# Block-causal attention followed by RWKV channel mix: queries kept in four classes from the scores to the normalization

## The chip, the cores and the metric

The kernel runs on one core of a Trainium2 chip. The metric is the time of one execution on the device, in microseconds (us). Before the change it is 314.23 us, the median of three executions (314.18 to 315.11 us). The profile is one execution, with a span of 312.8 us from the first to the last instruction.

Engines go by the names of the profile: PE is TensorE's matrix multiply, PEld its weight load, DVE is VectorE, ACT is ScalarE, POOL is GpSimd, and SP is SyncE, which issues the transfers. L657 means line 657 of the kernel.

## The reference

Two layers, one after the other. Inputs are float32; q, k and v have the shape (8 batches, 8 heads, 576 tokens, 64).

```python
# attention, causal in blocks of 64 tokens
scores = q @ k.T / sqrt(64)                       # 576 x 576 for each batch and head
scores = where(block(i) >= block(j), scores, -1e9)
attn   = exp(scores - max);  attn /= attn.sum(-1) + 1e-9
x      = attn @ v                                 # heads side by side: (8, 576, 512)

# channel mix
x_prev = x shifted by one token
xk = mu_k * x + (1 - mu_k) * x_prev
xr = mu_r * x + (1 - mu_r) * x_prev
out = sigmoid(xr @ w_r) * (relu(xk @ w_k)**2 @ w_v)   # (8, 576, 512)
```

The kernel takes no maximum off the scores, and it normalizes after the product with v: it computes the sums of the exponentials ("den") and the unnormalized values ("num") on PE, and multiplies num by 1/den on the way from PSUM to SBUF.

## The kernel before

Work is done per batch `b` and pair of heads `pr`. Scores are held transposed: keys on partitions, queries along the columns. Of the 576 queries the first 512 (`CUT`) are handled in `J = 4` classes: query 4p + j has position p (0 to 127) and class j. The last 64 are a block of their own. `M = 128` positions, `WD = M + 64`.

Two layouts of the transposed queries exist. In batches 0 and 1 (`b < TURNED`) PE does the transposing and the queries lie in token order, p outer and j inner. In batches 2 to 7 a transfer does it, and they lie in class order, j outer and p inner. Scores are always written to PSUM in token order:

```python
LATER = [                     # three score steps of one pair: (column, key chunk, first and last position)
    [(0, 0, 0, M)],                                   # 512 columns
    [(0, 0, M, WD), (D, 1, 32, M), (448, 1, M, WD)],  # 64, 384, 64
    [(0, 2, H2, M), (256, 2, M, WD), (320, 3, 96, M), (448, 3, M, WD)],   # 256, 64, 128, 64
]                             # batch 0 has 256+128+256+256+256+128 columns of the first kind, 1280 too
...
for p, col, kc, a, z in mms:
    for h in range(2):                       # the two heads, on partitions 0-63 and 64-127
        ...
        if a < M:
            moving = ask[:, J * a:J * z]
            dst = PS[:, h, col:col + J * w]
            if b >= TURNED:
                moving = ask[:, 0:CUT].rearrange("d (j p) -> d p j", j=J)[:, a:z]
                dst = dst.rearrange("k (p j) -> k p j", j=J)
            nc.tensor.matmul(dst, keys, moving, start=True, stop=True)      # L657
        else:
            nc.tensor.matmul(PS[:, h, col:col + D], keys, ask[:, CUT:S],    # L660
                             start=True, stop=True)
```

So in batches 2 to 7 consecutive columns of the moving operand are 128 bf16 elements, 256 bytes, apart.

ACT takes the exponential of two heads by 512 columns at a time into the float16 tile `e` (L679), POOL clears the part that the causal mask cuts off (L688), and PE makes sums and values from `e`, four heads side by side in four groups of 32 output columns (all through L721):

```python
def probs(b, head, kc, a, z):        # columns of e for the positions a to z
    ...
    return E[:, J * (a - a0):J * (z - a0)]

def sums(PS, a, z):                  # class j of head g goes to the partitions of its group that FOURTH picks
    for j in range(J):
        for kc in kcs:
            lo = max(a, kc * 32)
            for g in range(G):
                tiled(PS[:, lo - a:z - a], FOURTH[:, (J - j) % J:(J - j) % J + R],
                      probs(b, 4 * Q + g, kc, lo, z)[:, j::J], g, ...)
    ...                              # and the last 64 queries, with ONES

def part(PS, xs, a, z):              # values: 512 columns for each x, even and odd channels
    ...
    ps = ps[:, J * (lo - a):J * (z - a)]
    tiled(ps, V[:, kc, 4 * Q + g, x:D:2], probs(b, 4 * Q + g, kc, lo, z), g, ...)
```

In the sums the moving operand is every fourth float16 of `e`, 8 bytes apart. In the values it is contiguous. DVE then turns the sums into reciprocals, spreads the four classes over the partitions, and normalizes:

```python
nc.vector.reciprocal(tiles["c", key][:, 0:z - a], PS[:, 0:z - a])            # L772
nc.vector.reciprocal(tiles["rd", key][:, CUT:S], PS[:, M:WD])                # L775
...
for j in range(J):                                                          # L781
    nc.vector.stream_shuffle(tiles["rd", key][:, J * a + j:J * z:J],
                             tiles["c", key][:, 0:z - a], [j] * 32)
...
nc.vector.tensor_tensor(x, num, r.unsqueeze(1).to_broadcast(...), ALU.mult)  # L825, 512 tokens
nc.vector.tensor_tensor(x, num[:, 0:n * D]..., r[:, CUT:S]..., ALU.mult)     # L817, last 64
```

The spread writes each class into every fourth float32 of `rd`, 16 bytes apart. `x` is the float32 tile `xt` in token order, from which the channel mix follows: differences (L897), mixes (L910), the three products on PE (L948, L983, L1014).

The order of all instructions is fixed when the kernel is built, by a small planner that goes by an estimated duration for each step.

Of the kernel before, what the change touches and what calls it, by code (L numbers as in the profile page):

```python
# [20 lines left out]
TURNED = 2  # L21
# [259 lines left out]
def kernel(  # L281
# [24 lines left out]
    M = CUT // J  # L306
    WD = M + D
    JT = S // D
    CH = 512
    CHUNKS = [(0, CH // 2), (CH // 2, CH // 2)] + [  # L310
        (i * CH, CH) for i in range(1, B * S // CH)]
# [303 lines left out]
    def add_score(b, pr, i):  # L615


        sbuf = plan.buf("s")
        tail = i is None
        Q = pr // 2  # L620
        takes, uses = [sbuf], [tiles["qktbuf", b]]
        if tail:
            takes.append(el_buf[b][Q])
            deps = sum([evac[x, b, pr + y] for x in ("qkt", "tail")
                        for y in range(2)], [])
            if b:
                deps.append(ready["l", b - 1, Q])
            mms = [(pr + x, x * D, J, M, WD) for x in range(2)]
        else:
            mms = [(pr,) + p for p in pieces(b)[i]]  # L630
            deps = evac["qkt", b, pr] + (
                evac["tail", b, pr] if any(p[3] == M for p in mms) else [])
            if i == 0:
                tiles["ebuf", b, pr] = plan.buf("e")
                takes.append(tiles["ebuf", b, pr])
            else:
                uses.append(tiles["ebuf", b, pr])

        def fn():
            qkt = tiles["qkt", b]  # L640
            PS = tiles["ps", b, pr, i] = new("s", [P, 2, 512], FP)
            if i == 0:
                tiles["e", b, pr] = new("e", [P, 2, 3, 512], F16)
            for p, col, kc, a, z in mms:
                for h in range(2):
                    rows = slice(h * D, h * D + D)
                    keys, ask = qkt[rows, p, 1], qkt[rows, p, 0]
                    w = z - a
                    keys = keys[:, kc * P:kc * P + P]
                    if a < M:  # L650
                        moving = ask[:, J * a:J * z]
                        dst = PS[:, h, col:col + J * w]
                        if b >= TURNED:
                            moving = ask[:, 0:CUT].rearrange(
                                "d (j p) -> d p j", j=J)[:, a:z]
                            dst = dst.rearrange("k (p j) -> k p j", j=J)
                        nc.tensor.matmul(dst, keys, moving, start=True,  # L657
                                         stop=True)
                    else:
                        nc.tensor.matmul(PS[:, h, col:col + D], keys,  # L660
                                         ask[:, CUT:S], start=True, stop=True)
        pe = on("PE", 0.06 if tail else 0.215 + 0.02 * i, fn, deps, takes, uses,
                name=f"s{b}t{Q}" if tail else f"s{b}{pr}{i}", mode="rows",
                steps=2 * len(mms))
        if tail:
            def exl():
                nc.scalar.activation(
                    E4s[b % 2][0:D, 4 * Q:4 * Q + 4].rearrange(
                        "p (h a) q -> p h a q" if b < TURNED else
                        "p (a h) q -> p h a q", h=2),  # L670
                    tiles["ps", b, pr, i][0:D, :, 0:2 * D].rearrange(
                        "p h (a q) -> p h a q", q=D), AF.Exp, scale=ISQ)
            ready["l", b, Q] = on("ACT", 0.27, exl, [pe],
                                  uses=[sbuf, el_buf[b][Q]])
            return
        ebuf = tiles["ebuf", b, pr]

        def ex():
            nc.scalar.activation(tiles["e", b, pr][:, :, i, :],  # L679
                                 tiles["ps", b, pr, i], AF.Exp, scale=ISQ)  # L680
        t = on("ACT", 0.905, ex, [pe] + ([ready["x", b, pr, 0]] if i else []),
               uses=[sbuf, ebuf])
        ready["x", b, pr, i] = t

        def zero():
            for col, kc, a, z in pieces(b)[i]:
                if a == kc * 32 and a < M:
                    nc.gpsimd.memset(  # L688
                        tiles["e", b, pr][D:P, :, i, col:col + D], 0.0)
        n = sum(a == kc * 32 and a < M for col, kc, a, z in pieces(b)[i])  # L690
        if n:
            ready["z", b, pr, i] = on("POOL", 0.15 * n, zero, [t], uses=[ebuf])

    def probs(b, head, kc, a, z):


        if kc == J:
            return E4s[b % 2][:, head]
        i, col, a0, z0 = [
            (i, col, a0, z0) for i, piece in enumerate(pieces(b))  # L700
            for col, k0, a0, z0 in piece if k0 == kc and a0 <= a and z <= z0][0]
        pr, h = place(b, head)
        E = tiles["e", b, pr][:, h, i, col:]
        if a == M:
            return E[:, 0:D]
        return E[:, J * (a - a0):J * (z - a0)]

    def add_values(b, Q):

# [14 lines left out]
        def sums(PS, a, z):  # L724
            kcs = [kc for kc in range(J) if kc * 32 < z]
# [3 lines that stand above are left out]
                    for g in range(G):  # L729
                        tiled(PS[:, lo - a:z - a],  # L730
                              FOURTH[:, (J - j) % J:(J - j) % J + R],
                              probs(b, 4 * Q + g, kc, lo, z)[:, j::J], g,
                              (j, kc) == (0, kcs[0]), (j, kc) == (J - 1, kcs[-1]))
            for kc in range(J + 1) if z == M else ():
                for g in range(G):
                    tiled(PS[:, M:WD], ONES, probs(b, 4 * Q + g, kc, M, WD), g,
                          kc == 0, kc == J)

        def part(PS, xs, a, z):
            V = VOs[b % 2]  # L740
            wide = J * (z - a) if a < M else D
            for n, x in enumerate(xs):
                cols = slice(n * wide, n * wide + wide)
                kcs = [kc for kc in range(J) if kc * 32 < z] + [J] * (a == M)
                for kc in kcs:
                    lo = max(a, kc * 32)
                    for g in range(G):
                        ps = PS[:, cols]
                        if a < M:
                            ps = ps[:, J * (lo - a):J * (z - a)]  # L750
                        tiled(ps, V[:, kc, 4 * Q + g, x:D:2],
                              probs(b, 4 * Q + g, kc, lo, z), g,
                              kc == kcs[0], kc == kcs[-1])

        def group(name, a, z, deps, steps, dur, r_dur, s_dur):
# [11 lines left out]

            def recip():
                tiles["c", key] = new("c", [P, M], FP)
                tiles["rd", key] = new("rd", [P, S], FP)  # L770
                PS = tiles["den", key]
                nc.vector.reciprocal(tiles["c", key][:, 0:z - a],  # L772
                                     PS[:, 0:z - a])
                if z == M:
                    nc.vector.reciprocal(tiles["rd", key][:, CUT:S],  # L775
                                         PS[:, M:WD])
            t = on("DVE", r_dur, recip, [t], takes=[cbuf, rd], uses=[dbuf])

            def spread():
                for j in range(J):  # L780
                    nc.vector.stream_shuffle(  # L781
                        tiles["rd", key][:, J * a + j:J * z:J],
                        tiles["c", key][:, 0:z - a], [j] * 32)
            return rd, on("DVE", s_dur, spread, [t], uses=[cbuf, rd]), key

# [20 lines left out]
        def scale(t, i, xs, a, z, c, first, lo, hi, buf, rd, spr, key):  # L806
# [5 lines left out]
            def norm():  # L812
                x = xt_tile(c)[:, ch, 1 + off:1 + off + hi - lo]
                num, r = tiles["num", b, Q, i], tiles["rd", key]
                n = len(xs)
                if a == M:
                    nc.vector.tensor_tensor(  # L817
                        x, num[:, 0:n * D].rearrange("p (s t) -> p s t", s=n),
                        r[:, CUT:S].unsqueeze(1).to_broadcast([P, n, D]),
                        ALU.mult)  # L820
                    return
                num = num[:, 0:n * J * (z - a)].rearrange(
                    "p (s t) -> p s t", s=n)[:, :, lo - first:hi - first]
                r = r[:, lo - b * S:hi - b * S]
                nc.vector.tensor_tensor(  # L825
                    x, num, r.unsqueeze(1).to_broadcast([P, n, hi - lo]),
                    ALU.mult)
            dur = 0.2 if a == M else 0.00105 * (hi - lo) * len(xs) + 0.065
            xb = xtbuf[home]
            n = on("DVE", dur, norm, [t, spr], takes=[xb] if take else [],  # L830
# [294 lines left out]
```

## Time and profile before

| What | Value |
|---|---|
| time, median of 3 | 314.23 us |
| span of the profiled execution | 312.8 us |
| mean granted clock of PE | 0.989 |
| score matmuls of the four-class part (L657) | 272 records, 71.2 us busy |
| sums and values (L721), by `FOURTH` (sums) | 1088 records |
| exponentials (L679) | 96, 1024 ns each |
| reciprocals (L772), spread (L781) | 18 and 72 |
| normalization (L825) | 60, 23.6 us busy |
| clearing of `e` (L688) | 128, 205 ns each |
| read from HBM, written | 33.56 MB, 9.44 MB |

How to read it: a group's "busy" is the union of its records' time, so records that overlap are counted once, and the mean of a record can be longer than its share of the busy time. Consecutive instructions of one engine overlap at their ends; what one costs in a row of equals is the distance from its start to the next start. The first two heads' score matmuls run at the same time on the two halves of the partitions, and sums and values run four at a time on four column groups.

### The profile page before, as it was taken

The numbers are of one execution on the slowest core, as the hardware profiler recorded it, in microseconds if no ns is written. First come the engines' busy times: TensorE is split into PE (matmuls) and PEld (weight loads), VectorE is DVE, ScalarE is ACT, GpSimd is POOL, SyncE is SP. The second block draws the span as 40 slices with busy tenths as digits, with TensorE's granted clock in tenths as the row PEclk, the third lists the DMA queues.
The fourth block names the chain that finished last, engine by engine and source line by source line (L and its number), as shares of the span: only waits on it lengthen the run. The fifth ranks groups of instructions, "written<-read, shape, count | busy, mean of one in ns | idle before, by whom it ended". The sixth has DMA issues, their size and how long they took to land.

```text
span 312.8 us, 9964 instructions
## 1 busy us (share of the span) xinstructions
PE 294.1 (94%) x4120; PEld 139.5 (45%) x4120; DVE 220.5 (71%) x477; ACT 202.1 (65%) x313; POOL 114.1 (36%) x265
## 2 busy tenths in 40 slices
PE   1987799999999999899999999999999999999996
PEld 1664566344434345424344334443434354444443
DVE  3789999985198935991678817796587728999232
ACT  3868798868776678259761888538865766065360
POOL 3256559430431444343441574325451333000200
PEclk9998699999999999999999999999999999999999
DMA  7999979999999985893969339985942100020303
GB/s 259 308 262 246 245 229 242 256 227 227 263 200 205 234 195 105 190 256 82 206 131 254 126 68 208 188 234 131 173 85 72 69 2 2 34 103 0 137 0 134
DMA packets 118301, 51.51 MB, mean 165 GB/s; under 512 B 102768, under 2 KB 109168, under 8 KB 118256
## 3 DMA queue, kind: packets, MB, share of 16 engines
q1 hardware_dynamic: 118256, 50.88, 68.0%
q8 instruction: 32, 0.52, 0.7%
q14 instruction: 13, 0.11, 0.1%
HBM read 33.56 MB, written 9.44 MB: 137 GB/s over the span
## 4 chain that ended last, share of the span: by engine, by line
PE 80%; DVE 12%; ACT 4%; issue 2%; DMA 1%; SPq 0%; POOL 0%; DVEq 0%; ACTq 0%
PE t_mm L948 19%; PE t_s L657 17%; PE t_mm L1014 17%; PE t_mm L721 13%; PE t_mm L983 10%; DVE t_rd L781 5%; ACT t_e L679 3%; PE t_s L660 2%; DVE t_xt L825 2%; DMA t_ld<-in_q_dram 1%; PE t_mm L469 1%; DVE t_c L772 1%; DVE t_d L897 1%; DVE t_xk L910 1%; DVE t_rd L775 1%
## 5 line engine op out<-in xcount | busy, mean ns | idle before, releaser
L679 ACT ACTIVATE t_e<-t_s 128x1024 f16<-128x1024 f32 x96 | 95.1, 1024 | 53.6 <-PE t_s L660 26.6
L657 PE MATMUL t_s<-t_qkt 64*128 64x128 bf16 (+3 forms) x272 | 71.2, 588 | 1.5 <-ACT t_e L679 1.4
L948 PE MATMUL t_mm<-t_xk,WK 128*128 128x512 f16 (+1 forms) x320 | 69.1, 359 | 1.9 <-DVE t_xt L825 1.2
L1014 PE MATMUL t_mm<-WV,t_k 128*128 128x512 f16 (+1 forms) x296 | 66.1, 374 | 0.5 <-DVE t_o L1026 0.5
L688 POOL MEMSET t_e<- 64x128 f16 x128 | 24.0, 205 | 91.3 <-ACT t_e L679 89.6
L959 ACT ACTIVATE t_kr<-t_mm 128x512 f32<-128x512 f32 (+1 forms) x80 | 43.7, 560 | 18.5 <-PE t_mm L948 17.5
L948 PEld LDWEIGHTS <-WK 128*128 128x128 f16 x320 | 28.9, 98 | 38.7 <-issue 8.8
L1014 PEld LDWEIGHTS <-t_k 128*128 128x128 f16 x296 | 27.4, 98 | 38.4 <-issue 8.7
L772 DVE RECIPROCAL t_c<-t_mm 128x128 f32<-128x128 f32 (+1 forms) x18 | 15.6, 868 | 40.1 <-PE t_mm L721 40.0
L781 DVE STREAM_SHUFFLE t_rd<-t_c 128x128 f32<-128x128 f32 (+1 forms) x72 | 42.8, 868 | 0.0
L968 POOL TENSOR_TENSOR t_k<-t_kr 128x512 f16<-128x512 f32 (+1 forms) x27 | 26.1, 974 | 31.5 <-ACT t_kr L959 31.4
L983 PE MATMUL t_mm<-WR,t_xr 128*128 128x512 f16 x144 | 35.9, 380 | 0.0
L994 ACT ACTIVATE t_t<-t_mm 128x512 f32<-128x512 f32 x36 | 21.5, 600 | 20.5 <-PE t_mm L983 19.9
L968 DVE TENSOR_TENSOR t_k<-t_kr 128x512 f16<-128x512 f32 (+1 forms) x24 | 17.6, 743 | 23.1 <-ACT t_kr L959 23.1
L1026 DVE SCALAR_TENSOR_TENSOR t_o<-t_t,t_mm 128x512 f32<-128x512 f32 (+1 forms) x37 | 24.9, 681 | 12.5 <-PE t_mm L1014 9.6
L721 PE MATMUL t_mm<-t_e,VO 128*32 128x64 f16 (+4 forms) x1056 | 29.4, 251 | 2.1 <-DVE t_xt L825 1.0
L910 DVE SCALAR_TENSOR_TENSOR t_xk<-t_d,MUK,t_xt 128x512 f16<-128x512 f32 (+1 forms) x40 | 28.8, 747 | 1.7 <-POOL t_d L897 1.6
L910 DVE SCALAR_TENSOR_TENSOR t_xr<-t_d,MUR,t_xt 128x512 f16<-128x512 f32 (+1 forms) x40 | 29.8, 770 | 0.0
L660 PE MATMUL t_s<-t_qkt 64*128 64x64 bf16 x320 | 27.7, 204 | 1.1 <-ACT t_e L679 1.1
L825 DVE TENSOR_TENSOR t_xt<-t_mm,t_rd 128x448 f32<-128x448 f32 (+7 forms) x60 | 23.6, 436 | 4.1 <-PE t_mm L721 3.0
L657 PEld LDWEIGHTS <-t_qkt 64*128 64x128 bf16 x272 | 13.8, 101 | 27.5 <-issue 25.1
L721 PEld LDWEIGHTS <-VO 128*32 128x32 f16 x1184 | 19.4, 98 | 14.5 <-issue 6.5
(60 smaller groups left out, 291.0 us busy)
## 6 DMA issues: line engine op xcount, KB each, us to landing
out_dram<-t_o SPq DMA_DIRECT2D x35, 256.0 KB, 2.2
t_vl<-in_v_dram SPq DMA_DIRECT2D x32, 256.0 KB, 4.9
t_ld<-in_k_dram SPq DMA_DIRECT2D x48, 128.0 KB, 4.0
t_ld<-in_q_dram SPq DMA_DIRECT2D x24, 256.0 KB, 4.2
t_ld<-in_q_dram SPq DMA_DIRECT2D x8, 288.0 KB, 5.5
t_ld<-in_k_dram SPq DMA_DIRECT2D x8, 288.0 KB, 5.1
t_ld<-in_moe_w_k_dram SPq DMA_DIRECT2D x8, 256.0 KB, 5.0
t_ld<-in_moe_w_v_dram SPq DMA_DIRECT2D x8, 256.0 KB, 4.3
```

Source lines behind the costliest of these rows:

```text
L657: nc.tensor.matmul(dst, keys, moving, start=True, stop=True)
L660: nc.tensor.matmul(PS[:, h, col:col + D], keys, ask[:, CUT:S], start=True, stop=True)
L679: nc.scalar.activation(tiles["e", b, pr][:, :, i, :], tiles["ps", b, pr, i], AF.Exp, scale=ISQ)
L721: nc.tensor.matmul(ps[g * R:g * R + R], lhs, e, start=start, stop=stop, tile_position=(0, g * R))
L781: nc.vector.stream_shuffle(tiles["rd", key][:, J * a + j:J * z:J], tiles["c", key][:, 0:z - a], [j] * 32)
L825: nc.vector.tensor_tensor(x, num, r.unsqueeze(1).to_broadcast([P, n, hi - lo]), ALU.mult)
L910: nc.vector.scalar_tensor_tensor(tiles[name, h][:, cc, o:o + w], tiles["d", c, cc][:, 0:w], (MUK1, MUR1)[n][:, cc:cc + 1], xt_tile(c)[:, c ...
L948: nc.tensor.matmul(ps[:, 0:w], WK[:, cc, jc * P:(jc + 1) * P], tiles["xk", h][:, cc, o:o + w], start=(cc == 0), stop=(cc == CCn - 1))
L959: nc.scalar.activation(tiles["kr", c, jc][:, 0:w], tiles["pk", c, jc][:, 0:w], AF.Relu)
L968: (nc.vector if eng == "DVE" else nc.gpsimd).tensor_tensor(K2, KR, KR, ALU.mult)
L983: nc.tensor.matmul(ps, tiles["xr", h][:, cc, o + jt * P:o + (jt + 1) * P], WR[:, cc], start=(cc == 0), stop=(cc == CCn - 1))
L1014: nc.tensor.matmul(ps[:, 0:w], tiles["k2", h][:, jc, off:off + P], WV[:, jc, cols], start=(jc == 0), stop=(jc == JCn - 1))
```

## The change

The four classes stay apart from the scores on. The purpose is that PE reads contiguous columns in scores and sums; the return to token order moves to the normalization, which reads its operands from PSUM and SBUF across the classes.

- **Scores** are written to PSUM in class order inside each piece (j outer, position inner). In batches 2 to 7 the queries are then read contiguously. In batches 0 and 1 they are read every fourth bf16, 8 bytes apart.
- **Sums** read one class of `e` as a contiguous run. **Values** read and write class by class, in runs of 32 to 128 columns.
- **Clearing** of `e` covers the same number of elements in four runs of 16.
- **Spread** writes each class as a contiguous run of `rd`; the runs start 129 columns apart (`MP = M + 1`).
- **Normalization** walks positions and, inside, the four classes: num from PSUM at steps of z - a float32 (512 bytes for 128 positions), `rd` at steps of 129 float32 (516 bytes), and writes `x` contiguously as before.

```diff
+    MP = M + 1
...
-                        moving = ask[:, J * a:J * z]
-                        dst = PS[:, h, col:col + J * w]
-                        if b >= TURNED:
-                            moving = ask[:, 0:CUT].rearrange(
-                                "d (j p) -> d p j", j=J)[:, a:z]
-                            dst = dst.rearrange("k (p j) -> k p j", j=J)
-                        nc.tensor.matmul(dst, keys, moving, start=True,
-                                         stop=True)
+                        nc.tensor.matmul(
+                            PS[:, h, col:col + J * w].rearrange(
+                                "p (j n) -> p j n", j=J), keys,
+                            ask[:, 0:CUT].rearrange(
+                                "d (p j) -> d j p" if b < TURNED else
+                                "d (j p) -> d j p", j=J)[:, :, a:z],
+                            start=True, stop=True)
...
-                        tiles["e", b, pr][D:P, :, i, col:col + D], 0.0)
+                        tiles["e", b, pr][D:P, :, i, col:col + J * (
+                            z - a)].rearrange(
+                            "p h (j n) -> p h j n", j=J)[:, :, :, 0:D // J],
+                        0.0)
...
-        return E[:, J * (a - a0):J * (z - a0)]
+        return E[:, 0:J * (z0 - a0)].rearrange("p (j n) -> p j n", j=J)[
+            :, :, a - a0:z - a0]
...
-                              probs(b, 4 * Q + g, kc, lo, z)[:, j::J], g,
+                              probs(b, 4 * Q + g, kc, lo, z)[:, j], g,
...
-                            ps = ps[:, J * (lo - a):J * (z - a)]
+                            ps = ps.rearrange("q (j n) -> q j n", j=J)[
+                                :, :, lo - a:z - a]
...
-                tiles["rd", key] = new("rd", [P, S], FP)
+                tiles["rd", key] = new("rd", [P, J * MP + D], FP)
...
-                        tiles["rd", key][:, J * a + j:J * z:J],
+                        tiles["rd", key][:, j * MP + a:j * MP + z],
                         tiles["c", key][:, 0:z - a], [j] * 32)
...
+                p0, p1 = (lo - b * S) // J, (hi - b * S) // J
                 num = num[:, 0:n * J * (z - a)].rearrange(
-                    "p (s t) -> p s t", s=n)[:, :, lo - first:hi - first]
-                r = r[:, lo - b * S:hi - b * S]
-                nc.vector.tensor_tensor(
-                    x, num, r.unsqueeze(1).to_broadcast([P, n, hi - lo]),
-                    ALU.mult)
+                    "q (s j p) -> q s p j", s=n, j=J)[:, :, p0 - a:p1 - a]
+                r = r[:, 0:J * MP].rearrange("q (j p) -> q p j", j=J)[:, p0:p1]
+                x = x.rearrange("q s (p j) -> q s p j", j=J)
+                if n == 1:
+                    nc.vector.tensor_tensor(x[:, 0], num[:, 0], r, ALU.mult)
+                else:
+                    nc.vector.tensor_tensor(
+                        x, num, r.unsqueeze(1).to_broadcast(
+                            [P, n, p1 - p0, J]), ALU.mult)
```

Cuts are marked with "..."; the lines left out only rename the columns `CUT:S` of `rd` to `J * MP:`. The planner's durations are not touched.

More of the change, by code (lines that the diff above doesn't have):

```diff
@@ L774, in recip @@
                 if z == M:
-                    nc.vector.reciprocal(tiles["rd", key][:, CUT:S],
+                    nc.vector.reciprocal(tiles["rd", key][:, J * MP:],
                                          PS[:, M:WD])
@@ L818, in norm @@
                         x, num[:, 0:n * D].rearrange("p (s t) -> p s t", s=n),
-                        r[:, CUT:S].unsqueeze(1).to_broadcast([P, n, D]),
+                        r[:, J * MP:].unsqueeze(1).to_broadcast([P, n, D]),
                         ALU.mult)
                     return
+                p0, p1 = (lo - b * S) // J, (hi - b * S) // J
                 num = num[:, 0:n * J * (z - a)].rearrange(
-                    "p (s t) -> p s t", s=n)[:, :, lo - first:hi - first]
-                r = r[:, lo - b * S:hi - b * S]
-                nc.vector.tensor_tensor(
-                    x, num, r.unsqueeze(1).to_broadcast([P, n, hi - lo]),
-                    ALU.mult)
+                    "q (s j p) -> q s p j", s=n, j=J)[:, :, p0 - a:p1 - a]
[7 more added lines that the diff above has]
+                            [P, n, p1 - p0, J]), ALU.mult)
             dur = 0.2 if a == M else 0.00105 * (hi - lo) * len(xs) + 0.065
```

## The prediction, made before the changed kernel was run

> **What bounds the kernel now.** I read the page first, then the waits of PE from 60 us on, then stretches of the span, and last the timeline of single steps. The page says which engine is full and which one the end hangs on:
>
> ```profile
> PE 294.1 (94%) x4120; PEld 139.5 (45%) x4120; DVE 220.5 (71%) x477; ACT 202.1 (65%) x313; POOL 114.1 (36%) x265
> PE 80%; DVE 12%; ACT 4%; issue 2%; DMA 1%; SPq 0%; POOL 0%; DVEq 0%; ACTq 0%
> PE t_mm L948 19%; PE t_s L657 17%; PE t_mm L1014 17%; PE t_mm L721 13%; PE t_mm L983 10%; DVE t_rd L781 5%; ACT t_e L679 3%; PE t_s L660 2%; DVE t_xt L825 2%; DMA t_ld<-in_q_dram 1%; PE t_mm L469 1%; DVE t_c L772 1%; DVE t_d L897 1%; DVE t_xk L910 1%; DVE t_rd L775 1%
> ```
>
> PE carries 80% of the chain that ends last, and the four-class scores (L657) alone 17%, some 53 us. A busy PE can still be a waiting PE, so I look at what it waited for after 60 us (us in total, times, longest):
>
> ```profile
> PE t_mm L948 <- DVE t_xt L825: 1.2, 2, 0.7
> PE t_mm L721 <- DVE t_xt L825: 1.0, 1, 1.0
> PE t_mm L1014 <- DVE t_o L1026: 0.5, 1, 0.5
> PE t_mm L948 <- DVE t_o L1026: 0.4, 1, 0.4
> ```
>
> That is all: 3.1 us in 253. From 60 us on the order of work on PE is the time, and a microsecond taken out of PE is a microsecond off the end until another engine fills up. The stretches tell how near the others are (busy us and, last, clock, DMA share and GB/s):
>
> ```profile
> 0.00:60.00 60.00, 47.47 (x1138) 32.80 (x1142) 49.88 (x130) 46.03 (x77) 33.30 (x79) 0.94 0.98 258
> 60.00:240.00 180.00, 178.30 (x2363) 75.23 (x2356) 123.55 (x259) 121.39 (x181) 70.37 (x164) 1.00 0.81 179
> 240.00:313.00 73.00, 68.35 (x629) 31.43 (x626) 47.11 (x90) 34.70 (x57) 10.48 (x23) 1.00 0.14 52
> ```
>
> The columns are PE, PEld, DVE, ACT, POOL. The first 60 us are different: PE works 47 of 60 us and the transfers are at 0.98.
>
> [...]
>
> **Part 1, scores of batches 2 to 7.** One piece of 384 columns, in batch 1 (contiguous read) and in batch 3 (256-byte steps); columns are start, us, what:
>
> ```profile
> 37.32 0.33 PE L657 MATMUL t_s<-t_qkt 64*128 64x384 bf16 x2
> 37.48 0.19 PE L660 MATMUL t_s<-t_qkt 64*128 64x64 bf16 x2
> ```
>
> From start to next start, 0.16 us for 384 columns, 0.417 ns each. The two heads run side by side, so a piece counts once.
>
> ```profile
> 95.80 1.36 PE L721 MATMUL t_mm<-t_e,FOURTH 128*32 128x128 f16 x64
> 96.98 0.30 PE L721 MATMUL t_mm<-t_e,ONES 128*32 128x64 f16 x16
> ...
> 97.28 0.81 PE L657 MATMUL t_s<-t_qkt 64*128 64x384 bf16 x2
> 97.91 0.21 PE L660 MATMUL t_s<-t_qkt 64*128 64x64 bf16 x2
> ...
> 98.77 0.73 PE L721 MATMUL t_mm<-t_e,VO 128*32 128x512 f16 x16
> 99.43 1.02 PE L657 MATMUL t_s<-t_qkt 64*128 64x512 bf16 x2
> ```
>
> Here 97.28 to 97.91 is 0.63 us, 1.64 ns per column. A pair has 1280 such columns: 2.10 us before, 0.53 us after. With 4 pairs in 6 batches, 24 x 1.57 = **37.6 us off PE**, all behind 57 us, where the first scores of batch 2 start.
>
> **Part 2, sums.** The same fence has the sums of one group of four heads: 64 matmuls from 95.80 to 96.98, 1.18 us. The 16 value matmuls from 98.77 to 99.43 (512, 384, 256 and 128 columns, four heads) pass the same 5120 columns in 0.66 us. I checked that the larger number of matmuls is not what costs: 16 value matmuls of 64 columns take 0.13 us at 102.21, the same 0.13 ns per column. So it is the 8-byte step, and contiguous sums should take 0.66 us. Batch 0 splits its sums in two but has 5120 columns too. 16 groups x 0.52 = **8.3 us off PE**, about 6.5 of it after 60 us.
>
> **Part 3, scores of batches 0 and 1** now read at 8 bytes. The only measure for that step is the ratio of part 2, 1.8. I take it: 8 pairs x 0.53 x 0.8 = **3.4 us onto PE**, in the first 60 us, where PE has gaps.
>
> **Part 4, values** keep contiguous reads and writes, and the same columns: 0. **Clearing** has the same elements in shorter runs. It is 205 ns x 128 on an engine that is 36% busy, and PE waited for it once, 0.5 us: 0.
>
> **Part 5, spread.** Two of four in a row:
>
> ```profile
> 126.22 1.00 DVE L781 STREAM_SHUFFLE t_rd<-t_c 128x128 f32<-128x128 f32 x1
> ...
> 126.85 1.00 DVE L781 STREAM_SHUFFLE t_rd<-t_c 128x128 f32<-128x128 f32 x1
> ```
>
> 0.63 us from start to start. Those of 64 elements follow each other by 0.345 us (18.26, 18.60, 18.94), so (0.62 - 0.345)/64 = 4.3 ns per element. [...]so 0.20 us and 0.14 us: 56 x 0.42 + 16 x 0.21 = **27 us off DVE**. Only what stands in the chain counts. L781 has 5% of it, 15.6 us, but after 60 us PE works on beside those stretches, bar the waits of 3.1 us above. In the first 60 us three spreads stand in the chain with 5.6 us (18.1, 22.9 and 45.0 us); two thirds of that is 3.7 us, and part of it meets transfers at 0.98. Together with part 3 I take the first 60 us as 2 us shorter by the spreads and 2 us longer by the scores: nothing.
>
> **Part 6, normalization.** Rows by shape (busy us, mean ns of one):
>
> ```profile
> L825 DVE TENSOR_TENSOR t_xt<-t_mm,t_rd 128x448 f32<-128x448 f32 x8 | 4.9, 613 | 0.1
> ...
> L397 DVE COPY t_qkt<-t_mm 128x576 bf16<-128x576 bf16 x6 | 4.6, 779 | 4.6 <-PE t_mm L469 4.6
> ...
> L825 DVE TENSOR_TENSOR t_xt<-t_mm,t_rd 128x128 f32<-128x128 f32 x8 | 2.1, 281 | 0.0
> ```
>
> (613 - 281)/320 = 1.04 ns per element. The COPY row is the one case in which DVE already reads PSUM at a step: 576 elements, 128 bytes apart, started 0.67 us before its successor (14.79 to 15.46), 1.16 ns with the fixed part. So I expect PSUM at 512 bytes to be free. For `rd` in SBUF at 516 bytes there is no precedent. All slow cases here have steps that repeat the same place within 16 bytes: 256 bytes, 16 bytes, and 8 bytes by half as much. A step of 129 words does not; I read the odd number as chosen for that, and take **0**.
>
> **The sum.** PE: -37.6 - 8.3 + 3.4 = -42.5 us. After 60 us: 252.8 - 37.6 - 6.5 = 208.7 us of order on PE. In that stretch DVE would have 170.7 - 13 spreads x 1.7 = 149 us (71%) and ACT 156 us (75%). Transfers are the tight ones: 0.81 x 180 = 146 us of them must be done before the last scores. Those come at 259 us now and would come at about 215, 155 us after 60: 94%. Transposes of batch 3 are issued 15 to 21 us ahead of their scores (73.6, 84.4, 90.2, 95.3 against 94.8, 99.4, 106.1, 114.5), which buys some room. I add 7 us of new waits on transfers and on ACT: 314.2 - 37.6 - 6.5 + 7 = **277 us**.
>
> **Rivals.** *Transfers become the bound.* For it: 94%, and a share that is 0.98 to 60 us and reaches 1.12 from 80 to 100. Against it: PE waited for no transfer after 60 us, and from 140 us the share is 0.6 to 0.76, held back by consumers. It would give back some 15 us: 285 to 290. *DVE becomes the bound through the normalization.* If it paid 4.3 ns per element as the spread does, 16 x 1024 elements x 3.3 = 53 us more, DVE 220 - 27 + 53 = 247 us, with every mix behind it: 290 to 300. If it paid double, 17 us, it would be less than what the spread gives back, and hardly seen. *The exponentials take over.* ACT waited 47.8 us for scores; with quick scores its 1.02 us per step and two score buffers could hold PE. At 75% in total I give this 3 to 5 us, inside the 7. *Eight bytes cost as much as 256.* Then part 3 is 12.6 us instead of 3.4, half of it in gaps: 281. And *everything is hidden*, which 3.1 us of waits speak against.
>
> **Range and chances.** The bare PE sum without new waits is 270; with 267 as the lower end I allow some more from the spreads. Full transfers or a normalization at half rate with new waits lead to 290. Being no more than 2% faster would need over 36 of the 44 us to be lost. Faster 0.95, same 0.03, slower 0.02.
>
> **What would show it.** L657's 384-column piece at 0.16 us from start to start in batches 2 to 7 and about 0.3 us in batches 0 and 1; 64 `FOURTH` matmuls in 0.66 us; spreads 0.2 us apart; normalization rows still 1.04 ns per element; PE's waits after 60 us 5 to 12 us, led by transfers or ACT. Wrong would be: L825 rows two to four times as long, PE waiting long for t_xt or t_ld[...].

## The result and the profile after

The changed kernel takes **270.35 us** (median of four, 269.98 to 273.03), against 314.31 us before on the same chip: a ratio of 0.8615, with a 95% interval of 0.8557 to 0.8673. The profiled execution spans 268.2 us instead of 312.8. PE's granted clock was 0.994 (0.989 before). The prediction was 277 us, in a range of 267 to 290.

The same three lines of the page, after the change. Line numbers have moved: L652 are the four-class scores, L725 sums and values, L786 the spread, L833 and L835 the normalization, L822 that of the last 64 tokens, L958, L993 and L1024 the three products.

```profile
PE 249.5 (93%) x4120; PEld 130.6 (49%) x4120; DVE 203.5 (76%) x477; ACT 197.3 (74%) x313; POOL 117.6 (44%) x265
PE 70%; DVE 13%; ACT 6%; DMA 4%; POOL 3%; issue 2%; SPq 0%; DVEq 0%; POOLq 0%; ACTq 0%
PE t_mm L958 23%; PE t_mm L1024 16%; PE t_mm L993 12%; PE t_mm L725 9%; PE t_s L652 6%; ACT t_e L679 4%; DVE t_xt L833 3%; DMA t_qkt<-NB 3%; DVE t_xk L920 2%; PE t_s L660 2%; PE t_mm L470 2%; DVE t_rd L786 2%; DMA t_ld<-in_q_dram 2%; DVE t_d L907 2%; DVE t_c L777 1%
```

PE's busy time falls by 44.6 us, as much as the span. The scores go from 17% of the chain to 6%, and a new entry appears: the transposing transfer `t_qkt<-NB`, 3%. It is also the longest wait of PE after 60 us (total, times, longest):

```profile
PE t_s L652 <- DMA t_qkt<-NB: 2.7, 2, 2.4
PE t_mm L958 <- DVE t_xt L833: 1.7, 2, 1.2
PE t_mm L958 <- DVE t_o L1036: 0.4, 1, 0.4
```

4.8 us in all, against 3.1 before, and none of it for ACT. The timeline of PE (start, us, what) has the 384-column piece in batch 1 (8-byte steps now) and in batch 3 (contiguous now), and a group of 64 sum matmuls:

```profile
36.48 0.50 PE L652 MATMUL t_s<-t_qkt 64*128 64x384 bf16 x2
36.80 0.48 PE L660 MATMUL t_s<-t_qkt 64*128 64x64 bf16 x4
...
96.16 0.33 PE L652 MATMUL t_s<-t_qkt 64*128 64x384 bf16 x2
96.32 0.19 PE L660 MATMUL t_s<-t_qkt 64*128 64x64 bf16 x2
...
101.73 0.79 PE L725 MATMUL t_mm<-t_e,FOURTH 128*32 128x128 f16 x64
102.36 0.28 PE L725 MATMUL t_mm<-t_e,ONES 128*32 128x64 f16 x16
```

From start to next start: 0.32 us in batch 1 (0.16 before), 0.16 us in batch 3 (0.63 before), and 0.63 us for the sums (1.18 before). On DVE two shuffles of the spread now follow each other by 0.21 us instead of 0.63:

```profile
104.33 0.29 DVE L786 STREAM_SHUFFLE t_rd<-t_c 128x128 f32<-128x128 f32 x1
...
104.54 0.30 DVE L786 STREAM_SHUFFLE t_rd<-t_c 128x128 f32<-128x128 f32 x1
```

The normalization did not stay as it was. Rows by shape (busy, mean ns of one):

```profile
L833 DVE TENSOR_TENSOR t_xt<-t_mm,t_rd 128x448 f32<-128x448 f32 x8 | 7.5, 932 | 1.5 <-PE t_mm L725 1.4
...
L833 DVE TENSOR_TENSOR t_xt<-t_mm,t_rd 128x128 f32<-128x128 f32 x8 | 2.8, 368 | 0.0
```

(932 - 368)/320 = 1.76 ns per element, against 1.04 before. For 16 x 1024 elements that is 11.8 us more on DVE.

### The profile page after: what moved, and what is told of

Same layout as the page of the kernel before. It is cut to its first block, busy times and chain, and to the rows that moved or that the text cites. A ratio compares the mean times of both kernels' runs of the same rounds, so it can differ in the third digit from the quotient of the medians.

```text
span 268.2 us, 9965 instructions
## 1 busy us (share of the span) xinstructions
PE 249.5 (93%) x4120; PEld 130.6 (49%) x4120; DVE 203.5 (76%) x477; ACT 197.3 (74%) x313; POOL 117.6 (44%) x265
## 4 chain that ended last, share of the span: by engine, by line
PE 70%; DVE 13%; ACT 6%; DMA 4%; POOL 3%; issue 2%; SPq 0%; DVEq 0%; POOLq 0%; ACTq 0%
PE t_mm L958 23%; PE t_mm L1024 16%; PE t_mm L993 12%; PE t_mm L725 9%; PE t_s L652 6%; ACT t_e L679 4%; DVE t_xt L833 3%; DMA t_qkt<-NB 3%; DVE t_xk L920 2%; PE t_s L660 2%; PE t_mm L470 2%; DVE t_rd L786 2%; DMA t_ld<-in_q_dram 2%; DVE t_d L907 2%; DVE t_c L777 1%
## 5 line engine op out<-in xcount | busy, mean ns | idle before, releaser
L958 PE MATMUL t_mm<-t_xk,WK 128*128 128x512 f16 (+1 forms) x320 | 68.9, 359 | 2.8 <-DVE t_xt L833 1.7
L1024 PE MATMUL t_mm<-WV,t_k 128*128 128x512 f16 (+1 forms) x296 | 66.0, 374 | 0.0
L958 PEld LDWEIGHTS <-WK 128*128 128x128 f16 x320 | 29.0, 98 | 33.6 <-issue 3.6
L1024 PEld LDWEIGHTS <-t_k 128*128 128x128 f16 x296 | 27.4, 98 | 31.8 <-issue 2.2
L652 PE MATMUL t_s<-t_qkt 64*128 64x128 bf16 (+3 forms) x272 | 35.7, 327 | 4.8 <-DMA t_qkt<-NB 2.7
L993 PE MATMUL t_mm<-WR,t_xr 128*128 128x512 f16 x144 | 35.9, 380 | 0.0
L833 DVE TENSOR_TENSOR t_xt<-t_mm,t_rd 128x448 f32<-128x448 f32 (+6 forms) x56 | 30.7, 594 | 4.5 <-PE t_mm L725 4.2
L1036 DVE SCALAR_TENSOR_TENSOR t_o<-t_t,t_mm 128x512 f32<-128x512 f32 (+1 forms) x37 | 24.3, 665 | 8.2 <-PE t_mm L1024 7.6
L725 PE MATMUL t_mm<-t_e,VO 128*32 128x64 f16 (+4 forms) x1056 | 29.2, 251 | 0.4 <-issue 0.3
L978 DVE TENSOR_TENSOR t_k<-t_kr 128x512 f16<-128x512 f32 (+1 forms) x24 | 17.0, 720 | 15.8 <-ACT t_kr L969 15.6
L920 DVE SCALAR_TENSOR_TENSOR t_xr<-t_d,MUR,t_xt 128x512 f16<-128x512 f32 (+1 forms) x40 | 28.4, 735 | 0.0
L725 PEld LDWEIGHTS <-VO 128*32 128x32 f16 x1184 | 19.4, 98 | 10.8 <-issue 4.2
L660 PE MATMUL t_s<-t_qkt 64*128 64x64 bf16 x320 | 23.7, 197 | 0.6 <-ACT t_e L679 0.5
L652 PEld LDWEIGHTS <-t_qkt 64*128 64x128 bf16 x272 | 13.2, 96 | 17.2 <-issue 9.4
L993 PEld LDWEIGHTS <-t_xr 128*128 128x128 f16 x144 | 13.3, 98 | 16.1 <-issue 0.5
```

Source lines behind the costliest of these rows:

```text
L652: nc.tensor.matmul(PS[:, h, col:col + J * w].rearrange("p (j n) -> p j n", j=J), keys, ask[:, 0:CUT].rearrange("d (p j) -> d j p" if b < T ...
L725: nc.tensor.matmul(ps[g * R:g * R + R], lhs, e, start=start, stop=stop, tile_position=(0, g * R))
L833: nc.vector.tensor_tensor(x[:, 0], num[:, 0], r, ALU.mult)
L920: nc.vector.scalar_tensor_tensor(tiles[name, h][:, cc, o:o + w], tiles["d", c, cc][:, 0:w], (MUK1, MUR1)[n][:, cc:cc + 1], xt_tile(c)[:, c ...
L958: nc.tensor.matmul(ps[:, 0:w], WK[:, cc, jc * P:(jc + 1) * P], tiles["xk", h][:, cc, o:o + w], start=(cc == 0), stop=(cc == CCn - 1))
L978: (nc.vector if eng == "DVE" else nc.gpsimd).tensor_tensor(K2, KR, KR, ALU.mult)
```

## The experiments

### One part alone, from the kernel before

Each of three kernels has one change against the kernel before, with all else as it was. None brings every class to its right place, so they tell of times only.

```diff
 # p1_scores_only: queries read as they lie, contiguous, in batches 2 to 7
-                        if b >= TURNED:
+                        if False:
 # p2_sums_only: contiguous columns of e in the sums
-                              probs(b, 4 * Q + g, kc, lo, z)[:, j::J], g,
+                              probs(b, 4 * Q + g, kc, lo, z)[
+                                  :, j * (z - lo):(j + 1) * (z - lo)], g,
 # p3_spread_only: contiguous runs in the spread
-                        tiles["rd", key][:, J * a + j:J * z:J],
+                        tiles["rd", key][:, J * a + j * (z - a):
+                                         J * a + (j + 1) * (z - a)],
```

> The kernel before with one change: in batches 2 to 7 the queries of a score piece are read as contiguous columns instead of 256 bytes apart. Sums, spread and normalization stay as before; the classes are not sorted out, so the output is another one. Theory (PE's reading sets the time): 37.6 us less, about 277 us, and DVE's groups unchanged. Rival (the shorter DVE chain of spread and normalization brings the gain): 305 us or more, with PE waiting for t_xt.

> The kernel before with one change: the sums read contiguous float16 columns instead of every fourth, the same number of columns (which leaves out the right choice of class). Theory: 64 FOURTH matmuls take 0.63 us instead of 1.18, 16 groups, so 8.9 us less: about 305.5 us. Rival (sums are limited by the number of instructions or by weight loads): less than 3 us, 311 us or more.

> The kernel before with one change: the four shuffles of the spread write contiguous runs instead of every fourth float32 (the normalization then takes them in a wrong order; its time is as before). Theory: the shuffle falls from 0.62 to 0.2 us, DVE is 27 us less busy, but PE's order is the time: 2 to 4 us less, in the first 60 us, about 311.5 us. Rival (the chain that ended last had 5 per cent of the span in it): 10 us less, 304 us.

| Kernel | us, median | ratio to before (95%) | off before's 314.81 |
|---|---|---|---|
| scores only | 286.29 | 0.9090 (0.9066 to 0.9114) | 28.5 |
| sums only | 306.42 | 0.9722 (0.9692 to 0.9753) | 8.4 |
| spread only | 310.24 | 0.9856 (0.9834 to 0.9877) | 4.6 |

The sums bring what the columns say, 8.4 of 8.9 us. The same 64 matmuls, with the same weight loads, now take 0.62 us, so the rivals of instruction count and weight loads fall:

```profile
94.02 0.79 PE L721 MATMUL t_mm<-t_e,FOURTH 128*32 128x128 f16 x64
94.64 0.29 PE L721 MATMUL t_mm<-t_e,ONES 128*32 128x64 f16 x16
```

The spread alone brings 4.6 us, nearer to the theory's 2 to 4 than to the rival's 10. But most of it does not lie in the first 60 us: the first scores of batch 2 start only 0.9 us earlier (56.64 instead of 57.57 us), and the 3.1 us of PE's waits after 60 us are gone. The scores are the largest part, but bring 28.5 us instead of 37.6. What PE waits for after 60 us in that kernel says why, for the most part:

```profile
PE t_mm L948 <- DVE t_xt L825: 5.1, 4, 1.7
PE t_mm L1014 <- DVE t_xt L825: 1.9, 2, 1.4
PE t_mm L721 <- DVE t_xt L825: 1.6, 2, 1.0
```

With the five smaller ones it is 10.9 us instead of 3.1: 7.8 of the 9.1 us that are missing. Behind quick scores PE reaches the channel mix before reciprocal, spread and normalization have delivered: it waits 8.6 us for `t_xt` in these three lines, against 2.2 before, and DVE has 23% of the chain (12% before). So neither theory holds whole: PE's reading is most of it, and the slow spread comes onto the path once the scores are quick. That is a statement on the spread in the changed kernel, and was tested there.

### The spread put back into the changed kernel

```diff
-                        tiles["rd", key][:, j * MP + a:j * MP + z],
+                        tiles["rd", key][:, J * a + j:J * z:J],
...
-                r = r[:, 0:J * MP].rearrange("q (j p) -> q p j", j=J)[:, p0:p1]
+                r = r[:, 0:J * M].rearrange("q (p j) -> q p j", j=J)[:, p0:p1]
```

> The changed kernel with the spread put back: the shuffles write every fourth float32 (token order) and the normalization reads the reciprocals contiguously; num is still read from PSUM across the classes. The output is the reference's. New theory after the runs of the parts alone (with quick scores the slow spread comes onto the path): 8 to 10 us slower than the changed kernel, about 279 us, PE waiting some 8 us for t_xt. Rival (the spread is off the path in the changed kernel too): 273 us or less. Slope of the normalization: 1.76 ns per element if PSUM at 512 bytes costs, 1.04 if it was the reciprocals at 516 bytes.

280.39 us, ratio 0.8909 (0.8876 to 0.8942): **10.0 us more than the changed kernel** by the medians, 9.3 by the two ratios. DVE has 219.8 us of work instead of 203.5, and PE waits for it:

```profile
PE t_mm L958 <- DVE t_xt L833: 5.1, 4, 1.7
PE t_mm L1024 <- DVE t_xt L833: 2.8, 2, 2.0
PE t_mm L725 <- DVE t_xt L833: 1.4, 2, 1.0
...
PE t_mm L1024 <- DVE t_xt L822: 0.7, 1, 0.7
```

These are 10.0 us for `t_xt`, against 1.7 in the changed kernel: the theory holds. The 10.0 us are a net value, since the shuffles take 42.5 us here instead of 15.4, while the normalization gets shorter (613 instead of 932 ns for 448 elements, below).

The spread is thus worth 4.6 us alone and 10.0 us as the last part. Taken in one order the change splits into 28.5 us for the scores of batches 2 to 7, 5.9 us for everything else but the spread, above all the sums and the slower scores of batches 0 and 1 (286.29 to 280.39), and 10.0 us for the spread. That these add up to the whole says nothing, since each is a step to the next kernel. Another order would give other shares.

### Where the normalization's time comes from

The kernel with the spread put back still reads num from PSUM across the classes, but the reciprocals contiguously. Its rows:

```profile
L833 DVE TENSOR_TENSOR t_xt<-t_mm,t_rd 128x448 f32<-128x448 f32 x8 | 4.9, 613 | 0.1
...
L833 DVE TENSOR_TENSOR t_xt<-t_mm,t_rd 128x128 f32<-128x128 f32 x8 | 2.1, 277 | 0.0
```

(613 - 277)/320 = 1.05 ns per element, against 1.04 with contiguous reads in the kernel before: PSUM at 512 bytes costs nothing here. The opposite case, num contiguous and reciprocals at 516 bytes (tokens then come out in another order):

```diff
-                    "q (s j p) -> q s p j", s=n, j=J)[:, :, p0 - a:p1 - a]
+                    "q (s p j) -> q s p j", s=n, j=J)[:, :, p0 - a:p1 - a]
```

> The changed kernel, num read as contiguous columns from PSUM (tokens come out in another order), reciprocals still 516 bytes apart. One look at the normalization's slope: 1.04 ns per element if PSUM at 512 bytes is what costs in the changed kernel, 1.76 if it is SBUF at 516 bytes, between the two if each costs.

```profile
L833 DVE TENSOR_TENSOR t_xt<-t_mm,t_rd 128x448 f32<-128x448 f32 x8 | 7.4, 930 | 1.2 <-PE t_mm L725 1.0
...
L833 DVE TENSOR_TENSOR t_xt<-t_mm,t_rd 128x128 f32<-128x128 f32 x8 | 2.7, 364 | 0.0
```

(930 - 364)/320 = 1.77 ns, against 1.76 in the changed kernel. All of the extra time is the read of SBUF at 516 bytes. Whether the odd distance helps was a run of its own, `MP = M` in place of `MP = M + 1`:

> The changed kernel with the classes of the reciprocals 128 columns apart instead of 129, so 512 bytes. Theory (steps that repeat the place within 16 bytes are slow, as in the spread before with 4.3 ns): the normalization's slope goes to about 4 ns per element, DVE some 35 us busier, and the time to 285 us or more. Rival (the odd distance brings nothing): slope 1.76 and 270 us.

```profile
L833 DVE TENSOR_TENSOR t_xt<-t_mm,t_rd 128x448 f32<-128x448 f32 x8 | 7.5, 932 | 1.2 <-PE t_mm L725 1.0
...
L833 DVE TENSOR_TENSOR t_xt<-t_mm,t_rd 128x128 f32<-128x128 f32 x8 | 2.8, 366 | 0.0
```

271.98 us, ratio 0.8634 (0.8589 to 0.8679), and (932 - 366)/320 = 1.77 ns. My theory of steps that repeat a place within 16 bytes, a guess from the slow steps of the kernel before, falls: 512 and 516 bytes cost the same (1.77 and 1.76 ns), and the 129 columns bring nothing in this kernel.

Does the slower normalization cost time? Both operands were made contiguous (num as in the diff above, the reciprocals packed as in the spread-only kernel), so the classes are not put back in order:

> The changed kernel with one thing undone: the normalization reads num and the reciprocals as contiguous columns (the classes are not put back into token order, so the output is another one). Its slope should fall from 1.76 back to 1.04 ns per element, DVE 12 us less busy. Theory (DVE is off the path): 269 to 271 us, as the changed kernel with 270.35. Rival (the slower normalization holds the changed kernel back): 265 us or less.

```profile
L834 DVE TENSOR_TENSOR t_xt<-t_mm,t_rd 128x448 f32<-128x448 f32 x8 | 5.0, 620 | 1.3 <-PE t_mm L725 1.1
...
L834 DVE TENSOR_TENSOR t_xt<-t_mm,t_rd 128x128 f32<-128x128 f32 x8 | 2.1, 280 | 0.0
```

The slope is back at 1.06 ns ((620 - 280)/320) and DVE does 194.7 us of work, 8.8 less than in the changed kernel. Of the four executions (267.99, 271.69, 272.99 and 273.21 us) the last two, the profiled one among them, lie more than 1.5% above the fastest, and the ratio, 0.8569 (0.8498 to 0.8639), is of the first two alone. That interval takes in the changed kernel's ratio, so no gain can be shown; the rival's 265 us would be 0.842, below the interval. A gain of some 3 us is not excluded: 0.8498 would be 267.5 us.

### Writing at a step of 20 bytes

Since the step's repetition had fallen as the reason for slow reads, it was tried for the slow writes of the spread as well.

```diff
-                        tiles["rd", key][:, j * MP + a:j * MP + z],
+                        tiles["rd", key][:, 5 * a + j:5 * z:5],
...
+                r = r[:, 0:5 * M].rearrange(
+                    "q (p j) -> q p j", j=5)[:, p0:p1, 0:J]
```

> The changed kernel with the reciprocals interleaved again, but 5 columns to a position (four classes and a gap): the shuffles write float32 20 bytes apart, and the normalization reads runs of four. The output is the reference's. Theory A (a write is slow when it repeats the same place within 16 bytes): shuffles 0.2 us from start to start, normalization near 1.04 ns per element, DVE 12 us less busy than in the changed kernel, time 268 to 272 us as there. Theory B[...]: shuffles 0.6 us as before, about 280 us.

280.12 us, ratio 0.8916 (0.8873 to 0.8959), as with the spread put back. The shuffles again follow each other by 0.62 us:

```profile
45.25 1.00 DVE L786 STREAM_SHUFFLE t_rd<-t_c 128x128 f32<-128x128 f32 x1
...
45.87 1.02 DVE L786 STREAM_SHUFFLE t_rd<-t_c 128x128 f32<-128x128 f32 x1
```

Theory A falls: 16 and 20 bytes are equally slow to write (0.63 and 0.62 us). The times are those named for theory B, but what makes a stepped write slow was not shown: no step of less than 16 bytes was run. The normalization, which here reads runs of four, is at 1.04 ns ((611 - 279)/320).

### Batches 0 and 1, and the transfers

The scores of batches 0 and 1 were given contiguous reads (without sorting the queries there):

```diff
-                            ask[:, 0:CUT].rearrange(
-                                "d (p j) -> d j p" if b < TURNED else
-                                "d (j p) -> d j p", j=J)[:, :, a:z],
+                            (ask[:, J * a:J * z].rearrange(
+                                "d (j p) -> d j p", j=J) if b < TURNED else
+                             ask[:, 0:CUT].rearrange(
+                                "d (j p) -> d j p", j=J)[:, :, a:z]),
```

> The changed kernel, but in batches 0 and 1 the scores read the queries as contiguous columns (which leaves out their sorting into classes there; the same number of columns). The 384-column piece should go from 0.32 to 0.16 us in batches 0 and 1, 4.3 us less on PE in the first 60 us. Theory (in the first 60 us transfers and chains set the pace and PE has gaps): 1 to 2 us less, about 269 us. Rival (all of it counts): 266 us.

```profile
34.98 0.33 PE L652 MATMUL t_s<-t_qkt 64*128 64x384 bf16 x2
35.14 0.51 PE L661 MATMUL t_s<-t_qkt 64*128 64x64 bf16 x4
```

The piece takes 0.16 us again (34.98 to 35.14) and PE is busy 245.9 instead of 249.5 us. The four times are 268.94, 270.37, 272.62 and 273.17 us, with a median of 271.50 and a ratio of 0.8638 (0.8590 to 0.8687): no gain can be shown. The rival's 266 us, a ratio of 0.845, lies outside. The theory's 1 to 2 us would be lost in this scatter; in the two profiles the first scores of batch 2 start at 54.59 instead of 55.73 us, and the spans are 267.2 and 268.2 us.

The transfers of the changed kernel, in the same stretches as before but cut at 200 us (PE, PEld, DVE, ACT, POOL busy; clock, DMA share, GB/s):

```profile
0.00:60.00 60.00, 49.49 (x1164) 33.03 (x1165) 47.13 (x135) 48.16 (x81) 34.51 (x81) 0.97 1.01 258
60.00:200.00 140.00, 135.89 (x2324) 67.10 (x2323) 109.35 (x246) 113.70 (x175) 71.86 (x159) 1.00 1.10 224
```

By this share, 1.01 and 1.10, they have no slack left up to 200 us, but a share near 1 alone does not show that they hold anything up. To see what they cost, half of v was left out: heads 0 to 3 are loaded and used for heads 4 to 7 too, with the conversions as large as before.

```diff
-                         d[0:n], v[b, :, sc * P:sc * P + n].rearrange(
+                         d[0:n, 0:4], v[b, 0:4, sc * P:sc * P + n].rearrange(
...
-                convert(eng, VOs[b % 2][0:n, sc],
-                        tiles["vl", b, sc][0:n])
+                convert(eng, VOs[b % 2][0:n, sc].rearrange(
+                    "p (a h) d -> p a h d", a=2),
+                        tiles["vl", b, sc][0:n, 0:4].unsqueeze(1).to_broadcast(
+                            [n, 2, 4, D]))
```

> The changed kernel with half of v left out: heads 0 to 3 are loaded and used for heads 4 to 7 too, 4.7 MB and 18432 packets of 256 bytes fewer, conversions and PE work as they were. Theory (the transfers, at a share of 1.04 to 1.22 from 60 to 200 us, hold the changed kernel back by a few us and make its times scatter): 265 to 268 us, no wait for t_qkt, and a scatter under 1 us. Rival (PE and DVE alone set the time): 269.5 us or more.

> The kernel before with the same half of v left out. If the transfers were hidden there, as PE's waits say: within 2 us of 314.7. If they already set the pace of the first 60 us: 3 us or more less.

> The changed kernel with half of v left out and, in batches 0 and 1, the queries of the scores read as contiguous columns (4.3 us less on PE in the first 60 us, without the sorting into classes there). That shortening alone brought nothing (271.5 us). Theory (it was eaten by transfers): now it counts, 2 to 4 us less than with half of v left out alone. Rival (the first 60 us hang on other chains): same as that run within 1 us.

| Kernel with half of v | us, median | ratio to before (95%) |
|---|---|---|
| changed | 267.40 | 0.8508 (0.8479 to 0.8537) |
| before | 314.96 | 1.0004 (0.9986 to 1.0022) |
| changed, batches 0 and 1 contiguous | 268.07 | 0.8516 (0.8495 to 0.8538) |

The changed kernel with half of v, its stretches and then PE's waits after 60 us:

```profile
0.00:60.00 60.00, 50.00 (x1173) 32.74 (x1174) 48.88 (x138) 50.23 (x84) 34.74 (x84) 1.00 0.91 247
60.00:200.00 140.00, 137.34 (x2337) 67.65 (x2336) 110.34 (x256) 113.71 (x176) 70.07 (x160) 1.00 0.96 202
...
PE t_mm L960 <- DVE t_xt L835: 2.2, 3, 1.2
PE t_mm L727 <- issue: 0.9, 1, 0.9
PE t_mm L960 <- DVE t_o L1038: 0.4, 1, 0.4
```

In the kernel before, what was left out was hidden to within 0.2%. In the changed kernel it holds back about 3 us (270.35 - 267.40), and PE's wait for `t_qkt` is gone. Of the 3.1 us between the two spans (268.2 and 265.1) 1.9 lie ahead of the first scores of batch 2, which start at 53.87 instead of 55.73 us. The scatter stayed at 2.3 us, against what the theory said. The shorter scores of batches 0 and 1 bring nothing with fewer transfers either, so the 2 to 4 us of that theory did not come. As the transfers' share was still 0.90 in the first 60 us of that run, this does not clear them altogether: which chain holds the first 60 us stays open. No run beat the changed kernel with the whole of the computation in it.

## Why the prediction was right, and where it was not

**What bounds** (PE's order of work after 60 us): right. The first scores of batch 2 start at 55.73 us instead of 57.57, so 42.8 us of the span's 44.6 come after them. The steps take 24 x 1.57 + 12 x 0.55 = 44.3 us off PE there, and PE's waits grow by 1.7 us: 42.6. The waits came out at 4.8 us, just below the 5 to 12 forecast, and a transfer leads them as forecast.

**Part 1**: size right (0.16 us per piece). As a time it was right only because the spread changed too; alone it is 28.5 us. **Part 2**: 0.63 us against 0.66, 8.4 us alone. **Part 3**: the ratio was 2.0, not 1.8, so 4.3 us on PE instead of 3.4 by the length of the piece, and nothing of it can be shown in the time. **Part 4**: right; the clearing stayed at 203 ns, and the values (the rows with `VO`) at 29.2 us busy against 29.4, though they are now written in shorter runs.

**Part 5**: the size was right: the shuffles go from 42.8 to 15.4 us, 27.4 against 27. The 0.20 and 0.14 us for contiguous shuffles of 128 and 64 elements were an estimate, the normalization's 1.04 ns per element and the 0.07 us that 128 x 4.3 ns leave of 0.62; 0.21 and 0.14 us were measured. The failed step is "Only what stands in the chain counts", which I took to be nothing after 60 us. Alone, the spread already took away the 3.1 us of waits there. The chain of the kernel before cannot tell what would come onto it when the scores are quick; in the changed kernel this part is worth 10.0 us. The sum did not suffer, since it assumed that DVE would deliver in time, and with the quick spread it did.

**Part 6**: failed. I expected 1.04 ns; it is 1.76. PSUM is free, as I took it from the COPY row (1.05 ns at 512 bytes, 1.04 contiguous); the reciprocals in SBUF are not, and my reason, that an odd number of words avoids the cost, is refuted (1.76 ns at 516 bytes, 1.77 at 512). Of the rival "DVE becomes the bound" the milder form came: 11.8 us more work on DVE, less than the spread gives back, and no loss of time that could be shown.

**The sum**: the bare value without new waits was 270, and 270.35 was measured. The mis-sized term is the 7 us of new waits: PE's waits after 60 us rose by 1.7 us. The first 60 us, put at nothing, came out 1.8 us shorter. That these two cancel, so that the bare value fits to 0.4 us, is luck. The rival "transfers become the bound" had the right mechanism at about a fifth of its 15 us, by the run with half of v. Of the other rivals, the exponentials did not take over (PE waits for none after 60 us), and 8 bytes cost half of what 256 do (0.32 against 0.63 us for 384 columns).

## What to carry to other kernels

Look at the step of every operand in bytes, on the read and on the write side: one stepped operand made the scores on the busiest engine four times as long (0.63 against 0.16 us for 384 columns), and the row of the page that showed it looked like plain work. When a long step is moved, move it to where it is cheap: here to DVE's read of PSUM, which cost nothing (1.05 against 1.04 ns per element), and to an engine with time to spare (DVE was busy for 71% of the span, PE for 94%). And do not price the parts of a change one by one from the chain of the kernel before: a part that brings 4.6 us alone brought 10.0 us behind the others.

## What the runs showed of the hardware

- PE reading bf16 in SBUF, by the 384-column piece from start to next start: 0.42 ns per column contiguous (0.16 us, the kernel before in batch 1 and the changed one in batch 3), 0.83 at 8 bytes (0.32 us, the changed kernel in batch 1), 1.64 at 256 bytes (0.63 us, the kernel before in batch 3). No other step was run for bf16, and what causes the difference was not tested.
- DVE reading float32 in SBUF with each element far from the last: 1.76 ns per element at 516 bytes (the changed kernel), 1.77 at 512 (`MP = M`), against 1.05 contiguous (the spread put back). Runs of four, 20 bytes apart, are read at 1.04 (the step of 20 bytes). What causes the difference was not tested.
- DVE reading float32 in PSUM at 512 bytes: 1.05 ns per element (the spread put back), against 1.04 contiguous (the kernel before).
- DVE writing float32 in SBUF by shuffles, for 128 elements from start to next start: 0.63 us at 16 bytes (the kernel before), 0.62 at 20 bytes (the step of 20 bytes), 0.21 contiguous (the changed kernel).
